# Loading the first half of K in float32 over SyncE's queue and casting it on chip, in a fused attention and FFN kernel

## The chip, the cores and the metric

The kernel runs on one core of one Trainium2 chip. The metric is the device time of one execution in microseconds (us). Three runs of the kernel before took 511.74, 512.51 and 513.07 us; the median is 512.51 us. Engine names: PE is TensorE (PEld its weight loads), DVE VectorE, ACT ScalarE, POOL GpSimd, SP SyncE.

## The reference

```
k_proj = einsum('ks,bhsd->bhkd', E, k)          # E, F: 64 x 1024
v_proj = einsum('ks,bhsd->bhkd', F, v)          # q, k, v: 8 x 8 x 1024 x 64
scores = q @ k_proj^T / sqrt(64)                # per batch and head: 1024 x 64
attn   = softmax(scores, axis=-1)
x      = (attn @ v_proj), heads side by side    # 8192 x 512
h      = relu(x @ w_in)                         # w_in: 512 x 2048
out    = (h * h) @ w_out                        # w_out: 2048 x 512, out in float32
```

All inputs and the output are float32 in memory. The kernel computes in bfloat16 with float32 accumulation.

## The kernel before, in words

**Batches.** The eight batches are worked one after another. For each, the attention result xT (heads by tokens, bfloat16) feeds an FFN in two chunks of 512 tokens. While PE runs the FFN of batch b, the attention stages of batch b+1 and the projections of batch b+2 are put between its matmuls by a plan written out by hand (`at(step, ...)`, L461 to L514): the FFN is a generator of steps, and after step n the stages planned for n are issued. The order on PE is the order of the program text; the other engines' orders follow from it.

**Opening.** Batch 0 has no earlier FFN to hide under, so its attention runs ahead of all else (L428 to L455). E is loaded in float32 by SP (L87) into a tile of `soft_pool` with the tag "rs" (three buffers, also used by the inverse of the softmax sums), cast to bfloat16 by DVE (L429), and transposed on PE (`projection`, L132, with a DVE copy at L138). `project_k(0)` (L191 to L197) multiplies ET with the first four heads of K (8 matmuls at L194), `project_k(1)` does the other four. `transpose_q_chunk` (L227), `transpose_k` (L210), `chunk_scores` (L322), `chunk_sums` (L328), `project_v` (L199) and `chunk_values` (L333) follow for the first chunk of 512 tokens in groups of four heads. `warm(n)` (L141) issues n matmuls on zeros.

**First FFN chunk of batch 0.** `Ffn.steps` with `cold` set: the first matmuls are at L358 (input weights, `w_in`), ReLU on ACT (L354) and square on DVE (L355), then second matmuls (L364) with `w_out` in four pieces. The last piece, `w_out_131` in the profile, is first used at step 23, where the plan also holds the second chunk's scores.

**Queues.** Nearly all loads are issued by POOL (`load`, L75), since POOL's transfers cast float32 to bfloat16 on the way. Their order at the start is: K heads 0 to 3, Q heads 0 to 3 (half of the tokens), F, K heads 4 to 7, Q heads 4 to 7 (half), V heads 0 to 3, V heads 4 to 7, then five pieces of w_in, three of w_out, the rest of Q, the last of w_out, and the whole K, V and Q of the batches 1 and 2. At most eight of POOL's transfers are under way: the ninth waits for the first to land, the tenth for the second, and so on. SP issues E, and later the stores of the output (L373, the first at 44.02 us) and the transposing DMAs.

The part around the change reads:

```
for g in range(2):
    load(K0[:, half[g]], tokens(k, 0, h=half[g]))
    load(Q0[:, half[g], 0:4, :], tokens(q, 0, h=half[g], i=slice(0, 4)))
    if g == 0:
        make_identity(nc, ident[:])
        load(f_bf[:], F[:])
```

Of the kernel before, what the change touches and what calls it, by code (L numbers as in the profile page):

```python
# [8 lines left out]
P = 128  # L9
F32 = mybir.dt.float32  # L10
# [8 lines left out]
def kernel(  # L19
# [11 lines left out]
    nc = tc.nc  # L31

    B, H, S, D = q.shape
# [5 lines left out]
    NI = 8  # L39
# [18 lines left out]
    soft_pool = ctx.enter_context(tc.tile_pool(name="soft", bufs=3))  # L58
# [10 lines left out]
    def bank(shape=(P, 512), dtype=F32):  # L69
        return fps.tile(list(shape), dtype, tag="bank", name="ps_bank")  # L70

    def tokens(src, b, h=slice(None), i=slice(None)):
        return src[b].rearrange("h (p i) d -> p h i d", i=NI)[:, h, i, :]

    def load(t, src):  # L75
        return nc.gpsimd.dma_start(t, src)  # L76
# [9 lines left out]
    e_f32 = soft_pool.tile([KP, S], F32, tag="rs", name="e_f32")  # L86
    nc.sync.dma_start(e_f32[:], E[:])  # L87

    K0, Q0, V0 = (qkv_pool.tile([P, H, NI, D], BF16, name=n) for n in ("K_sb", "Q_sb", "V_sb"))
    f_bf = soft_pool.tile([KP, S], BF16, tag="expT", name="f_bf")  # L90
    half = (slice(0, 4), slice(4, 8))
    ident = const_pool.tile([P, P], BF16, name="ident")
    for g in range(2):
        load(K0[:, half[g]], tokens(k, 0, h=half[g]))
        load(Q0[:, half[g], 0:4, :], tokens(q, 0, h=half[g], i=slice(0, 4)))
        if g == 0:
            make_identity(nc, ident[:])
            load(f_bf[:], F[:])
# [13 lines left out]
    for lo, hi in W_IN_PIECES:  # L112
        t = wpool.tile([P, NCB, (hi - lo) * P], BF16, name=f"w_in_{lo}")
# [4 lines left out]
    for j in range(WP):  # L118
        if j == WP - 1:
            load(Q0[:, :, 4:8, :], tokens(q, 0, i=slice(4, 8)))  # L120
        t = wpool.tile([P, fn, DM], BF16, name=f"w_out_{j}")
# [10 lines left out]
    def projection(name, e_bf):  # L132
        ps = bank([P, NI, KP], BF16)
        view = e_bf[:].rearrange("k (p i) -> k i p", i=NI)
        for i in range(NI):
            nc.tensor.transpose(ps[:, i, :], view[:, i, :], ident[0:KP, 0:KP])
        t = const_pool.tile([P, NI, KP], BF16, name=name)
        nc.vector.tensor_copy(t[:], ps[:])  # L138
        return t

    def warm(n):  # L141

        ps = bank()
        for _ in range(n):
            nc.tensor.matmul(ps[:], lhsT=zeros[:, 0:P], rhs=zeros[:], start=True, stop=True)
# [281 lines left out]
    with tc.manual_schedule(engines={PE}):  # L427
        e_bf = soft_pool.tile([KP, S], BF16, tag="expT", name="e_bf")  # L428
        nc.vector.tensor_copy(e_bf[:], e_f32[:])  # L429
        warm(8)  # L430
        ET = projection("ET", e_bf)
        warm(4)
        att = Attention(0)
        att.project_k(0)
        warm(1)
        att.transpose_q_chunk(0, Q0, 0)
        att.transpose_k((0,))
        warm(3)
        att.chunk_scores(0, 0)
        FT = projection("FT", f_bf)  # L440
        warm(3)
        att.project_k(1)
        att.chunk_sums(0, 0)
        att.transpose_q_chunk(0, Q0, 1)
        att.transpose_k((1,))
        warm(2)
        att.chunk_scores(0, 1)
        warm(2)
        att.project_v(0)
        warm(1)  # L450
        att.chunk_sums(0, 1)
        att.chunk_values(0, 0)
        warm(1)
        att.project_v(1)
        att.chunk_values(0, 1)  # L455

        coming = None
        for b in range(B):
            plan = {}

            def at(step, fn, *args, **kwargs):  # L461
                plan.setdefault(step, []).append(lambda: fn(*args, **kwargs))

            if b == 0:
                at(21, att.transpose_q_chunk, 1, Q0, 0)
                at(21, att.transpose_q_chunk, 1, Q0, 1)
                at(23, att.chunk_scores, 1, 0)
                at(23, att.chunk_scores, 1, 1)
                at(25, att.sums, 0)
                at(27, att.chunk_values, 1, 0)  # L470
                at(27, att.chunk_values, 1, 1)
                nxt = Attention(1)
                nxt.load()
            if b + 1 < B:
                if b + 2 < B:
                    coming = Attention(b + 2)
                    coming.load()
                if b == 0:
                    at(36, nxt.project)
                    at(39, nxt.transpose_q, 0)  # L480
                    at(39, nxt.transpose_q, 1)
                    at(39, nxt.transpose_k)
                    at(41, nxt.scores, 0)
                    at(41, nxt.scores, 1)
                    at(44, nxt.transpose_q, 2)
                    at(44, nxt.transpose_q, 3)
                    at(45, nxt.sums, 0)
                    at(48, nxt.values, 0, True)
                    at(48, nxt.scores, 2)
                    at(51, nxt.values, 1)  # L490
                    at(51, nxt.scores, 3)
                    at(55, nxt.sums, 2)
                    at(55, nxt.values, 2)
                    at(55, nxt.values, 3, True)
                else:
                    at(14, nxt.scores, 0)
                    at(14, nxt.scores, 1)
                    at(18, nxt.sums, 0)
                    at(18, nxt.values, 0, True)
                    at(18, nxt.scores, 2)  # L500
                    at(27, nxt.values, 1)
                    at(27, nxt.scores, 3)
                    at(49, nxt.sums, 2)
                    at(49, nxt.values, 2)
                    at(49, nxt.values, 3, True)
                if b + 2 < B:
                    if b == 0:
                        at(61, coming.project)
                        at(63, coming.transpose_q_dma)
                        at(64, coming.transpose_k)  # L510
                    else:
                        at(27, coming.project)
                        at(30, coming.transpose_q_dma)
                        at(29, coming.transpose_k_dma)  # L514
            for step, _ in enumerate(Ffn(att, b == 0).steps(), 1):
                for stage in plan.pop(step, []):
                    stage()
            assert not plan, plan
            att, nxt = nxt, coming
# [30 lines left out]
```

## Time and profile before

| what | value |
|---|---|
| profiled execution, device time | 511.74 us |
| its span, first to last instruction | 510.0 us |
| median of three runs | 512.51 us |
| PE busy | 497.0 us, 97% |
| ACT, DVE, POOL busy | 272.4, 216.7, 32.0 us |
| DMA, POOL's queue | 29.49 MB in 30880 packets |
| DMA, SP's queue | 23.99 MB in 36928 packets |
| read from memory | 59.24 MB |

The profile is of one execution, which was also the quickest of the three; 1.74 us of its time lie outside the span. The bytes of POOL's queue are counted in bfloat16, after the cast: twice 29.49 MB and E's 0.26 MB make the 59.24 MB that were read. A rate of 208 GB/s on that queue is thus 416 GB/s of reading.

A row of the timeline gives start, length, engine, line, operation, tiles and count; in brackets is how long the engine sat idle before it and what ended that. A POOL or SP row of a DMA is its issue; its landing is told by the view of the tile.

### The profile page before, as it was taken

To read this page: it belongs to the slowest core of one execution; us is meant where nothing else is said; L and a number is where in the kernel's file an instruction comes from. 1 tells how busy PE (TensorE), PEld (TensorE's weight loads), DVE (VectorE), ACT (ScalarE), POOL (GpSimd) and SP (SyncE) were. 2 spreads that over 40 slices of the span, in tenths; PEclk is the share of its full clock that TensorE was granted. 3 is DMA by queue.
4 is the path that set the end of the run, shared out by engine and by line. 5 is a ranking of instruction groups with operands and counts; after the bars stand their busy time and mean duration, and the time that the engine had idled before them with its cause. 6 is when DMAs were issued, how large, how long until landed. Compare 5 with 4: busy or idle time off the path is not lost.

```text
span 510.0 us, 6889 instructions
## 1 busy us (share of the span) xinstructions
PE 497.0 (97%) x2710; PEld 222.8 (44%) x2761; DVE 216.7 (42%) x437; ACT 272.4 (53%) x411; POOL 32.0 (6%) x44
## 2 busy tenths in 40 slices
PE   8799999999999999999999999999999999999997
PEld 4344444444444444444444444444444444444444
DVE  2442766444434445235452345444443443522130
ACT  2564484664718556374645736366472755544351
POOL 7320100121000020001000000000000000000000
PEclk9999999999999999999999999999999999999999
DMA  9999999899996199104931060101102011010102
GB/s 156 204 205 222 226 207 202 132 220 207 195 217 125 56 185 201 65 0 126 181 78 42 17 160 1 62 22 42 53 1 82 1 41 42 31 54 21 63 0 82
DMA packets 67840, 53.92 MB, mean 106 GB/s; under 512 B 29152, under 2 KB 59616, under 8 KB 67808
## 3 DMA queue, kind: packets, MB, share of 16 engines
q0 software_dynamic: 30880, 29.49, 36.8%
q1 hardware_dynamic: 36928, 23.99, 17.5%
q8 instruction: 21, 0.34, 0.3%
q14 instruction: 11, 0.09, 0.1%
HBM read 59.24 MB, written 16.78 MB: 149 GB/s over the span
## 4 chain that ended last, share of the span: by engine, by line
PE 88%; DMA 7%; issue 2%; POOL 1%; ACT 1%; DVE 1%; POOLq 0%; ACTq 0%
PE ps_bank L364 41%; PE ps_bank L358 40%; DMA w_out_131<-in_moe_w_out_dram 4%; DMA w_in_116<-in_moe_w_in_dram 3%; PE ps_bank L185 2%; PE ps_att L256 1%; PE ps_att L290 1%; PE ps_att L312 1%; PE ps_bank L312 1%; DVE rs L300 0%; PE ps_bank L241 0%; DVE xT L341 0%; POOL K_sb L76 0%; POOL V_sb L76 0%; ACT expT L270 0%
## 5 line engine op out<-in xcount | busy, mean ns | idle before, releaser
L355 DVE TENSOR_TENSOR hsq<-h_relu 128x512 bf16<-128x512 bf16 x256 | 108.9, 426 | 192.9 <-ACT h_relu L354 192.0
L354 ACT ACTIVATE h_relu<-ps_bank 128x512 bf16<-128x512 f32 x256 | 151.7, 599 | 69.3 <-PE ps_bank L358 69.2
L364 PEld LDWEIGHTS <-hsq 128*128 128x128 bf16 x1040 | 99.5, 98 | 123.6 <-issue 9.3
L371 ACT COPY o_sb<-ps_bank 128x512 f32<-128x512 f32 (+1 forms) x65 | 37.6, 579 | 119.7 <-PE ps_bank L364 110.9
L364 PE MATMUL ps_bank<-w_out_124,hsq 128*128 128x512 bf16 (+1 forms) x257 | 65.6, 376 | 0.2
L364 PE MATMUL ps_bank<-w_out_131,hsq 128*128 128x512 bf16 (+1 forms) x251 | 64.1, 376 | 1.4 <-issue 1.1
L364 PE MATMUL ps_bank<-w_out_128,hsq 128*128 128x512 bf16 (+1 forms) x252 | 64.3, 376 | 1.1 <-issue 1.0
L364 PE MATMUL ps_bank<-w_out_126,hsq 128*128 128x512 bf16 (+1 forms) x249 | 64.2, 376 | 1.1 <-issue 0.8
L300 DVE COPY rs<-rs 32x1024 f32<-32x1024 f32 x60 | 41.3, 689 | 47.2 <-ACT rs L295 45.8
L358 PE MATMUL ps_bank<-xT,w_in_122 128*128 128x512 bf16 x255 | 58.9, 380 | 0.0
L358 PE MATMUL ps_bank<-xT,w_in_118 128*128 128x512 bf16 x250 | 57.7, 380 | 0.4
L358 PE MATMUL ps_bank<-xT,w_in_120 128*128 128x512 bf16 x247 | 57.4, 379 | 0.4
L270 ACT ACTIVATE expT<-ps_att 128x1024 bf16<-128x1024 f32 x32 | 31.8, 1024 | 18.1 <-PE ps_att L256 18.1
L358 PEld LDWEIGHTS <-w_in_120 128*128 128x128 bf16 x256 | 24.9, 98 | 30.4 <-issue 0.4
L358 PEld LDWEIGHTS <-w_in_118 128*128 128x128 bf16 x256 | 24.9, 98 | 30.2 <-issue 0.4
L358 PEld LDWEIGHTS <-w_in_122 128*128 128x128 bf16 x256 | 24.4, 98 | 31.1 <-issue 2.7
L358 PE MATMUL ps_bank<-xT,w_in_114 128*128 128x512 bf16 x128 | 30.6, 379 | 0.3 <-DVE xT L341 0.2
L358 PE MATMUL ps_bank<-xT,w_in_116 128*128 128x512 bf16 x126 | 30.0, 379 | 0.1
L294 ACT ACTIVATE rs<-ps_att 128x1024 f32<-128x1024 f32 x15 | 15.3, 1023 | 12.7 <-PE ps_att L290 12.7
L316 DVE TENSOR_TENSOR xT<-ps_att,rs 128x512 bf16<-128x512 f32 x28 | 18.1, 686 | 8.7 <-PE ps_att L312 8.4
L358 PEld LDWEIGHTS <-w_in_114 128*128 128x128 bf16 x128 | 12.4, 98 | 15.6 <-issue 1.3
L358 PEld LDWEIGHTS <-w_in_116 128*128 128x128 bf16 x128 | 12.5, 98 | 15.2 <-issue 0.2
(71 smaller groups left out, 233.9 us busy)
## 6 DMA issues: line engine op xcount, KB each, us to landing
out_dram<-o_sb SPq DMA_DIRECT2D x63, 256.0 KB, 2.0
K_sb<-in_k_dram POOLq DMA_DIRECT2D x7, 1024.0 KB, 22.1
V_sb<-in_v_dram POOLq DMA_DIRECT2D x7, 1024.0 KB, 26.7
Q_sb<-in_q_dram POOLq DMA_DIRECT2D x7, 1024.0 KB, 15.0
K_sb<-in_k_dram POOLq DMA_DIRECT2D x2, 512.0 KB, 7.1
V_sb<-in_v_dram POOLq DMA_DIRECT2D x2, 512.0 KB, 12.0
Q_sb<-in_q_dram POOLq DMA_DIRECT2D x2, 256.0 KB, 7.6
w_in_118<-in_moe_w_in_dram POOLq DMA_DIRECT2D x1, 512.0 KB, 15.5
```

Of the source, the lines that this page charges most:

```text
L185: nc.tensor.matmul(ps[LO, :], lhsT=ET[:, i, :], rhs=self.K[:, :, i, :], start=f, stop=l)
L256: nc.tensor.matmul(ps[o, par], lhsT=self.kT[r, h % 4, h // 4, :], rhs=self.qT[r, h, n, :], start=True, stop=True)
L270: nc.scalar.activation(e[:], ps[:], AF.Exp, scale=SCALE)
L294: nc.scalar.activation(rs[1][:], ps[:], AF.Ln)
L300: nc.vector.tensor_copy(rs[j][lack:lack + 32], rs[j][have:have + 32])
L312: nc.tensor.matmul(ps_x[par][o], lhsT=self.vp[r, 2 * pr + a, :], rhs=e[r, par], start=True, stop=True)
L316: nc.vector.tensor_tensor(out=self.xT[:, pr, :, par], in0=ps_x[par].rearrange("p (c t) -> p c t", c=2), in1=rs[:, par].rearrange("p (c t) ...
L354: nc.scalar.activation(r[:], ps[:], AF.Relu)
L355: nc.vector.tensor_tensor(out=self.hsq[c][:, fb, :], in0=r[:], in1=r[:], op=ALU.mult)
L358: nc.tensor.matmul(ps[:], lhsT=w_in_blk(cb, fb), rhs=self.xT[:, cb, c].rearrange("p a t -> p (a t)"), start=(cb == 0), stop=(cb == NCB - 1),)
L364: nc.tensor.matmul(ps[:, m], lhsT=self.hsq[c][:, fb, tb * P:(tb + 1) * P], rhs=w_out_blk(fb)[:, m], start=(fb == 0), stop=(fb == NFB - 1),)
L371: nc.scalar.copy(o[:, m], ps[:, m])
```

## The change

The first half of K (heads 0 to 3 of batch 0, 1 MB of float32) is no longer loaded by POOL with a cast. SP issues it behind E in two float32 transfers of two heads each, into two tiles of the tag "rs". DVE casts the first (heads 0 and 1) ahead of its copy of ET, ACT the second (heads 2 and 3) ahead of its copy of the projected K, into the same K tile. POOL's first transfer is now Q. All else is as before.

```
@@ -86,12 +86,19 @@
+    k_f32 = []
+    for j in range(2):
+        t = soft_pool.tile([P, 2, NI, D], F32, tag="rs", name="k_f32")
+        nc.sync.dma_start(t[:], tokens(k, 0, h=slice(2 * j, 2 * j + 2)))
+        k_f32.append(t)
...
     for g in range(2):
-        load(K0[:, half[g]], tokens(k, 0, h=half[g]))
+        if g == 1:
+            load(K0[:, half[g]], tokens(k, 0, h=half[g]))
...
         nc.vector.tensor_copy(e_bf[:], e_f32[:])
+        nc.vector.tensor_copy(K0[:, 0:2], k_f32[0][:])
+        nc.scalar.copy(K0[:, 2:4], k_f32[1][:])
         warm(8)
```

## Prediction

> **What bounds the kernel now.** I read the page's first lines, then the timeline of the opening, the waits, and the DMA rate in fine slices.
>
> ```profile
> PE 497.0 (97%) x2710; PEld 222.8 (44%) x2761; DVE 216.7 (42%) x437; ACT 272.4 (53%) x411; POOL 32.0 (6%) x44
> ```
>
> PE is busy for 497.0 of 510.0 us, so nearly all of its idle time can only lie in the opening, the part that the change touches. The timeline there:
>
> ```profile
> 0.74 0.57 SPq L87 DMA_DIRECT2D e_f_91<-in_E_dram  x1
> 1.25 0.89 POOL L76 DMA_DIRECT2D K_sb<-in_k_dram  x1 [0.80 <-POOLq L534]
> 2.14 0.76 POOL L76 DMA_DIRECT2D Q_sb<-in_q_dram  x1
> ...
> 4.37 0.81 DVE L429 CAST e_bf<-e_f_91 64x1024 bf16<-64x1024 f32 x1 [3.15 <-DMA e_f_91<-in_E_dram]
> ...
> 5.95 0.42 DVE L138 COPY ET<-ps_bank 128x512 bf16<-128x512 bf16 x1 [0.77 <-PE ps_bank L136]
> ...
> 7.32 1.03 PE L194 MATMUL ps_bank<-K_sb,ET 128*64 128x256 bf16 x8 [0.44 <-DMA K_sb<-in_k_dram]
> ...
> 14.62 1.06 ACT L276 ACTIVATE rs<-rs 128x1024 f32<-128x1024 f32 x1
> ...
> 19.74 1.06 PE L204 MATMUL ps_bank<-V_sb,FT 128*64 128x256 bf16 x16 [1.44 <-DMA V_sb<-in_v_dram]
> ...
> 42.35 1.02 PE L364 MATMUL ps_bank<-w_out_131,hsq 128*128 128x512 bf16 x4 [0.19 <-DMA w_out_131<-in_moe_w_out_dram]
> ```
>
> PE waits for three transfers in turn: 0.44 us for the first half of K (7.32), 1.44 us for the last half of V (19.74), and 0.19 us for the last piece of w_out (42.35). The last row decides. From 19.74 to 42.35 PE's own work and the stream of loads run side by side, and they arrive within 0.19 us of each other. To end sooner the kernel needs both: PE earlier at the FFN, and w_out_131 (issued 22.1, landing 20.2 us later at 42.3) earlier. After 42.35 no transfer holds PE up again. So the change is worth the **smaller** of two advances, x of PE and y of the stream. The stream is full almost from the start, shown in 40 slices of 0.1 us from 2 to 6 us:
>
> ```profile
> GB/s 82 328 205 0 0 41 0 246 287 492 410 369 236 72 62 21 10 61 61 143 154 174 215 184 184 205 236 195 205 225 205 195 195 225 164 143 154 184 174 184
> ```
>
> E's float32 comes at about 400 GB/s around 3 us. POOL's transfers count bytes after the cast, so their 205 means 410 GB/s read: the same ceiling. Between them is a hole, 3.3 to 4.0 us, with a mean of 61.
>
> **The change, part by part.**
>
> *The stream, y.* Bytes read stay the same: 1.05 MB of K takes 2.5 to 2.6 us at 410 GB/s either way. What can move is idle time. The K transfers stand in SP's queue right behind E; E's bytes begin about 1.3 us after its issue, and at 0.57 us each SP has issued both K transfers by 2.45, so their bytes follow E's without a break, while POOL's Q begins about when K did, near 3.3. The hole closes: 0.7 us x (1 - 61/208) = 0.5 us. Against it: float32 written at full width, and two queues mixed. The nearest row is a store beside POOL's loads: near 48 us, six slices of 0.25 us stand at a mean of 282 GB/s; a store's 262 KB over 1.5 us is 175 of it, which leaves 107 of loads, or 214 read: 389 moved in place of 410, 5% lost, and the two queues share about evenly. Over some 4 us of mixing that is 0.2 us, and 0.3 at the 8% by which 4 to 12 us (190 GB/s) falls short of 205 to 209 later. I take 0.15, since K comes first and mixes for less. Upward bound: the hole and also this early shortfall made good, 0.5 + 8% of 8 us = 1.1. So y is 0.35; if the hole stays and the 0.3 is lost, -0.3; at best +1.1.
>
> The Trainium skill, "DMA: Bandwidth & Descriptors", Rules for kernel authors, speaks against the change: spreading transfers over several issuing engines gives no bandwidth, since all share 16 DMA engines; only issue time is saved. By it y is 0, for the 0.89 us of POOL's issue saved is not on the path. It is a rule for a running stream; the hole above is a starting one, and I go by the hole.
>
> *PE's way to the FFN, x.* Removed: the 0.44 us wait for K at 7.32. Added: K's second tile, then ACT's cast, and only then L194. Landing: bytes from 3.2. If K has the engines alone, they end at 5.8; if it shares evenly with Q (0.52 MB read), at 7.1. E landed at 0.74 + 3.6 = 4.3, about 0.8 us after its bulk ended, so K lands at 6.6 to 7.9. The cast of 128x1024 on ACT isn't in the trace; the nearest row, L276 of that shape from SBUF, is 1.06 us. L194 starts at 7.7 to 9.0 instead of 7.32, d = 0.4 to 1.7; I take 1.0, the middle: the store's row speaks for even sharing, K's place ahead of Q for the engines alone. DVE's cast of the first tile (the e_bf row, 0.81 us: time goes by elements in a row) stands ahead of the ET copy, which PE needs: at a landing of 5.0 to 6.6 it ends at 5.8 to 7.4 and ET at 6.2 to 7.9, before ACT's cast ends. Behind ACT's cast is only the copy of the projected K (L174), which needs L194 anyway.
>
> From L194 to the wait for V, PE runs back to back (2.95 us busy of 9 to 12, 5.78 of 12 to 18.3), so d is handed on, less about 0.1 where it stood for other landings. It arrives before V's last half at 18.3 + 0.9 = 19.2; V landed at 19.7. So the 1.44 us idle swallows the delay. V moves with the stream: 19.35. Also, V's second half came 3.7 us after the first (15.98 to 19.7) where 0.52 MB at 208 GB/s take 2.5; one 16 KB instruction fetch lies in 13 to 26 us and may have held one engine up. If it falls elsewhere, V lands near 18.2 and PE's 19.2 decides. So x is 0.4 to 0.5, between 0 (d = 1.6) and 1.4 (d = 0).
>
> *The rest, at nothing.* POOL has one transfer fewer and issues each of the others up to 0.89 us earlier; the eight-under-way rule keeps pairing the same transfers from the tenth on, so the stream is fed as before. SP's next work is the store at 44.02. The two new tiles take the "rs" buffers, first wanted again at 13.57, after both casts. Warm-up matmuls are unchanged. If cover is gone, ACT's cast costs 1.06.
>
> *Sum.* min(x, y) = 0.35: 511.74 - 0.35 = 511.4 for the profiled execution, the fastest of three. On the median 512.51, 0.77 above it, that is **512.1 us**.
>
> **Rivals**, on the median too.
>
> 1. *Nothing gained:* y is 0, as w_out_131 lands when it did; mixing eats the hole, or the stall of one engine by an instruction fetch sets the landing. For it: the landing is set by the slowest of 16 engines. PE gains at most the 0.19 of its wait: 512.4. Against it: the hole is real idle time of all engines.
> 2. *Slower: K late.* If POOL's packets get two turns in three, K crawls from 3.2 at half its rate or less, 205 GB/s: 5.1 us, bytes end at 8.3, landed 9.1, cast done 10.2, L194 at 10.3, d = 3.0. It decides from d = 1.6, L194 at about 8.9. Price d - 1.6 = 1.4: 513.9. For it: stores between 44 and 54 us land 5.4 to 7.0 us after issue, held behind POOL's loads, against 2.0 in the middle of all. Against: K enters engines that hold nothing of POOL's yet. With it comes a second price: PE idles from about 6.9 to 10.3. The trace shows 1.4 us of idle (18.3 to 19.7) at a granted clock of 1.00; the first eight matmuls of 512 columns take 3.59 us, later four 1.04, so a fallen clock would double PE's work for some us: up to 2 more, 515.9.
> 3. *More gained:* y = 1.1 and V not held up, d at 0.4: 511.4.
>
> The Trainium skill, "TensorE: Matmul & The Clock Gate", What's actually happening, lets the clock fall only after an idle window of some 3.4 us. By it the forecast's gap (about 7 to 8.3) leaves the clock alone, and rival 2 stands at its edge. No row here shows a fall.
>
> **How the numbers follow.** Forecast 0.45, rival 1 0.22, rival 2 0.18, rival 3 0.15. Runs of one kernel spread from 511.74 to 513.07, so about 0.3% (1.5 us) is what can be told from no change. The range takes in rival 3 less half of that spread (511.4 - 0.6) and rival 2's first price with a little of it: 510.8 to 514.2. Faster by over 0.3% needs more than every advance found: 0.06, by rival 3 and spread. Slower by over 0.3%, above 514.0, takes rival 2 at its dear end: 0.13. Within: 0.81.
>
> **What would show it.** In the profile after: no hole at 3.3 to 4.0 us in the DMA slices; K's second tile landing at 6.6 to 7.9; ACT's cast about 1.06 us; L194 at 7.7 to 9.0; L204's second batch at 18.9 to 19.5; the wait at w_out_131 still there, and its row at about 42.0. It would be wrong if L194 came after 9, if w_out_131 landed no earlier, or if w_out_131 no longer ended any wait and the time still moved.

## The result and the profile after

| kernel | median | lowest to highest | runs |
|---|---|---|---|
| before | 513.13 us | 511.74 to 513.28 | 6 |
| after | 514.75 us | 514.05 to 516.43 | 6 |

The changed kernel is slower: ratio **1.0041**, 95% interval 1.0023 to 1.0059. That is 1.6 us on the medians, and 2.3 us between the two profiled executions, each of them the quickest of its kernel (514.05 and 511.74).

PE's busy slices on the page of before, then the span, PE's busy slices and the granted clock on the page of after (40 slices each, in tenths):

```profile
PE   8799999999999999999999999999999999999997
```
```profile
span 512.3 us, 6897 instructions
...
PE   5999999999999999999999999999999999999997
...
PEclk7999999999999999999999999999999999999999
```

PE's slices differ in the first two alone, so the 2.3 us lie in the opening. Its timeline answers to the rows that the prediction showed of before:

```profile
1.37 0.57 SPq L92 DMA_DIRECT2D k_f_93<-in_k_dram  x1
1.99 0.45 SPq L92 DMA_DIRECT2D k_f_95<-in_k_dram  x1
...
5.61 0.69 DVE L437 CAST K_sb<-k_f_93 128x1024 bf16<-128x1024 f32 x1 [0.42 <-DMA k_f_93<-in_k_dram]
...
9.24 1.04 ACT L438 CAST K_sb<-k_f_95 128x1024 bf16<-128x1024 f32 x1 [7.21 <-DMA k_f_95<-in_k_dram]
10.34 1.86 PE L201 MATMUL ps_bank<-K_sb,ET 128*64 128x256 bf16 x8 [3.45 <-ACT K_sb L438]
...
16.52 1.06 PE L201 MATMUL ps_bank<-K_sb,ET 128*64 128x256 bf16 x8
...
22.58 1.06 PE L211 MATMUL ps_bank<-V_sb,FT 128*64 128x256 bf16 x16
...
44.85 1.03 PE L371 MATMUL ps_bank<-w_out_134,hsq 128*128 128x512 bf16 x4
```

The two tiles of K were issued 0.6 us apart and landed 3.6 us apart: DVE's cast of the first waited until 5.61, ACT's of the second until 9.24. PE then stood still for 3.45 us, and began the first K product at 10.34 instead of 7.32. Its eight matmuls took 1.86 us, not 1.03: the clock had fallen. The last two rows have no bracket. Nothing waits for V or for the last piece of w_out any more; PE comes later than both.

The windows of after show the clock; the columns are the window, its length, PE, PEld, DVE, ACT and POOL busy, the granted clock, the DMA share and GB/s. They are cut at the instants at which the clock's record changes:

```profile
4.07:7.49 3.42, 2.08 (x14) 0.98 (x13) 1.71 (x3) 0.00 (x0) 3.42 (x5) 1.00 1.21 293
7.49:10.90 3.41, 0.56 (x3) 0.48 (x3) 0.00 (x0) 1.04 (x1) 2.08 (x3) 0.50 1.19 233
10.90:14.31 3.41, 3.41 (x22) 2.03 (x20) 1.09 (x3) 0.36 (x1) 1.48 (x2) 0.50 1.32 202
14.31:17.72 3.41, 3.36 (x33) 1.90 (x32) 0.74 (x4) 1.02 (x1) 0.74 (x1) 1.00 1.26 204
```

Half clock lasts two windows, 7.49 to 14.31. In the first PE mostly waits; in the second it works at half speed throughout. So the product of the second half of K, which in before stands at 12.11,

```profile
12.11 1.06 PE L194 MATMUL ps_bank<-K_sb,ET 128*64 128x256 bf16 x8
```

is at 16.52: the 3.02 us have become 4.41. By the second product with V (22.58 against 19.74) it is 2.84, because V's idle time of 1.44 us is swallowed, and at the last piece of w_out 2.50 (44.85 against 42.35). From there on the offset stays: 2.50 up to about 150 us and 2.45 from 175 us to the last of these matmuls, as PE hardly idles there.

The DMA rate of after from 2 to 6 us, in slices of 0.1 us:

```profile
GB/s 82 369 164 0 41 0 0 0 369 410 369 451 389 226 164 246 225 184 246 205 205 307 369 369 410 430 410 389 410 348 236 195 210 195 189 195 205 200 200 225
```

Up to 4.9 us all of this is float32, so 410 is full rate. The hole of before, 3.3 to 4.0, is half filled: a mean of 213 GB/s. From 4.9 on the bytes are POOL's, counted after the cast, so 200 is full rate again.

### The profile page after: what moved, and what is told of

Same layout as the page of the kernel before. It is cut to its first block, busy times and chain, and to the rows that moved or that the text cites. A ratio compares the mean times of both kernels' runs of the same rounds, so it can differ in the third digit from the quotient of the medians.

```text
span 512.3 us, 6897 instructions
## 1 busy us (share of the span) xinstructions
PE 497.9 (97%) x2710; PEld 223.8 (44%) x2761; DVE 217.2 (42%) x438; ACT 273.7 (53%) x412; POOL 31.4 (6%) x43
## 4 chain that ended last, share of the span: by engine, by line
PE 93%; issue 2%; DVE 1%; DMA 1%; ACT 1%; SPq 0%; DVEq 0%; ACTq 0%
PE ps_bank L365 43%; PE ps_bank L371 41%; PE ps_bank L192 2%; PE ps_att L263 1%; DMA k_f_95<-in_k_dram 1%; PE ps_att L319 1%; PE ps_att L297 1%; DVE xT L348 1%; PE ps_bank L319 1%; PE ps_bank L201 1%; PE ps_bank L152 1%; PE ps_bank L238 0%; PE ps_bank L248 0%; ACT expT L277 0%; DVE rs L307 0%
```

## The experiments

The theory, from the two traces: the second tile of K lands late because SP's queue has to take turns with POOL's loads (the cause), and PE's wait for it costs twice, once as delay and once as lost clock. The rivals: float32 or the casts themselves cost; Q's issue ahead of the tile alone is to blame; the lost clock does not matter, or is all that matters.

**The second tile through ACT's queue** (e1).

```
-        nc.sync.dma_start(t[:], tokens(k, 0, h=slice(2 * j, 2 * j + 2)))
+        (nc.sync if j == 0 else nc.scalar).dma_start(t[:], tokens(k, 0, h=slice(2 * j, 2 * j + 2)))
```

> Only the issuing engine of the second K tile changes: ACT's queue, at about 0.75 us, in place of SP's third place at 1.99. Theory (order of arrival): the tile came late, at 9.2 us, because its packets reached the DMA engines just behind those of POOL's Q and then took turns with POOL's. Ahead of Q it should land at 6.0 to 7.0, the first L194-type matmul (L201) start at 7.1 to 8.1, the granted clock stay at 1.00 and the time come back to within 0.5 us of before (0.999 to 1.001). Rival (rate): float32 in 2 KB packets over a hardware queue is slow in itself, and E and the first tile beside it make it worse: the tile lands at 8.5 or later and the time stays about 1.003 to 1.004 of before.

512.58 us (511.82 to 514.33, 12 runs), ratio 0.9995 [0.9983, 1.0008]. The loss is gone in the median, yet not in the execution that was profiled, its slowest. The timeline of that one:

```profile
4.63 1.04 ACT L438 CAST K_sb<-k_f 128x1024 bf16<-128x1024 f32 x1 [2.61 <-DMA k_f<-in_k_dram]
6.09 0.68 DVE L436 CAST e_bf<-e_f 64x1024 bf16<-64x1024 f32 x1 [4.88 <-DMA e_f<-in_E_dram]
9.17 0.69 DVE L437 CAST K_sb<-k_f 128x1024 bf16<-128x1024 f32 x1 [2.40 <-DMA k_f<-in_k_dram]
```

By the starts of the casts, ACT's tile lands first, at 4.6; E lands by 6.1, against 4.5 in after; and now SP's tile of K is the late one, at 9.2. In both kernels the third float32 transfer to land is the late one. Neither the size of the tiles nor the number of casts changed, so the casts are not the price of the change.

**Twenty warm-up matmuls** ahead of the first K product in place of four (e2).

```
-        warm(4)
+        warm(20)
```

> The changed kernel with 20 warm-up matmuls instead of 4 ahead of project_k(0), so that PE works through the wait. The landing of K and the cast stay: L201 at 10.3. Theory: the late K costs 3.0 us at L201 and the fallen clock another 1.4 by the second half of K; without the fall the FFN starts at about 23.1 in place of 24.5 and the time is 1.3 to 1.5 us below the changed kernel, about 1.001 to 1.002 of before. Rival (clock): the fallen clock is the whole loss, since V's wait swallows the rest; then the time is within 0.3 us of before. If the clock plays no part, the time stays at 1.003 to 1.004.

514.18 us (513.04 to 514.73), ratio 1.0023 [1.0011, 1.0034]. In the profiled execution the clock rose only at 10.47, so the twenty took 6.75 us and put the product itself off to 12.55, past K. They are too many to tell the clock's share; n5 below has fewer.

**Q behind the identity** (e3): POOL's first load is moved behind `make_identity`.

```
-        load(Q0[:, half[g], 0:4, :], tokens(q, 0, h=half[g], i=slice(0, 4)))
         if g == 0:
             make_identity(nc, ident[:])
+        load(Q0[:, half[g], 0:4, :], tokens(q, 0, h=half[g], i=slice(0, 4)))
+        if g == 0:
             load(f_bf[:], F[:])
```

> POOL issues its first Q load behind the making of the identity, some 0.5 us later than in the changed kernel; nothing else moves. Theory (order of arrival): the second K tile's packets now enter before Q's and follow the first tile's: landing at 6.3 to 7.2 in place of 9.2, L201 at 7.4 to 8.3, clock 1.00, time 0.999 to 1.001 of before. Rival (rate): half a microsecond of head start changes the landing by no more than that, 8.7 or later, and the time stays at about 1.003.

514.63 us (513.94 to 515.82), ratio 1.0035 [1.0022, 1.0048]. It tells nothing of the order: Q's issue moved only from 1.25 to 1.28 us. It stands as a second measurement of after: the second tile landed at 9.46, though in its profile DVE cast K's first tile ahead of E.

**Heads 2 and 3 back to POOL** (e4): SP loads one float32 tile, POOL the other two heads, as its first load, with the cast.

```
-    for j in range(2):
+    for j in range(1):
...
-        if g == 1:
-            load(K0[:, half[g]], tokens(k, 0, h=half[g]))
+        h0 = slice(2, 4) if g == 0 else half[1]
+        load(K0[:, h0], tokens(k, 0, h=h0))
...
-        nc.scalar.copy(K0[:, 2:4], k_f32[1][:])
```

> Only heads 0 and 1 come in float32 over SP, cast by DVE; heads 2 and 3 come by POOL with its cast, as its first load; ACT's cast is gone. Theory: POOL's piece follows the float32 piece in the engines and lands at 6.3 to 7.0, L201 starts at 6.9 to 7.1, at or before the 7.32 of before. The stream of loads, a little ahead as the hole after E is filled, sets the end: 0.2 to 0.5 us below before, 0.999 to 1.000. Rival (any float32 K beside POOL is a loss): L201 at 8 or later and the time above 1.002.

512.16 us (511.31 to 514.26, 12 runs), ratio **0.9985 [0.997, 0.9999]**: faster than before, by 0.77 us on the medians, with an interval that just clears 1. The timeline of its profiled execution (513.28 us, one of its slower ones):

```profile
5.80 0.92 DVE L437 CAST K_sb<-k_f 128x1024 bf16<-128x1024 f32 x1 [0.66 <-DMA k_f<-in_k_dram]
...
7.10 1.06 PE L201 MATMUL ps_bank<-K_sb,ET 128*64 128x256 bf16 x8 [0.25 <-DVE ET L145]
...
19.49 1.06 PE L211 MATMUL ps_bank<-V_sb,FT 128*64 128x256 bf16 x16 [1.34 <-DMA V_sb<-in_v_dram]
42.35 1.02 PE L371 MATMUL ps_bank<-w_out,hsq 128*128 128x512 bf16 x4 [0.43 <-DMA w_out<-in_moe_w_out_dram]
```

PE waits for no K at all, only for ET. The waits for V and w_out are back, and the last row is at 42.35, exactly where before had it: the stream decides again. So one float32 tile and its cast are harmless, and the second tile behind it is the harm. Where the 0.77 us come from, this profile does not show, as its opening ends no sooner than in the profile of before.

**Q 0.4 us later** (e5): a memset on POOL ahead of its first load.

```
+    pause = const_pool.tile([P, 1024], F32, name="pause")
+    nc.gpsimd.memset(pause[:], 0.0)
```

> The changed kernel with POOL filling a 128x1024 float32 tile of zeros ahead of its first load, so that Q and all behind it are issued about 1 us later or more. (The earlier attempt at this moved Q's issue by 0.03 us only and told nothing.) Theory (order of arrival): the second K tile's packets now reach the engines before Q's and follow the first tile's without the pause of 1 us: landing at 6.3 to 7.5 in place of 9.2, L201 at 7.4 to 8.6. The time is then 0.999 to 1.001 of before, unless the stream runs dry behind K. Rival (the hardware queue): SP's third transfer is late whatever POOL does, landing 8.5 or later, time 1.003 or more.

513.88 us (512.52 to 514.9), ratio 1.0009 [0.9993, 1.0024]. Q's issue moved to 1.63, and the second tile began right behind the first; but in the profiled execution ACT's cast still had to wait until 9.48:

```profile
9.48 1.04 ACT L441 CAST K_sb<-k_f 128x1024 bf16<-128x1024 f32 x1 [7.46 <-DMA k_f<-in_k_dram]
10.57 1.86 PE L204 MATMUL ps_bank<-K_sb,ET 128*64 128x256 bf16 x8 [3.77 <-ACT K_sb L441]
```

This does not settle the order, though. The profiled execution is the slowest of the twelve, and its packet records have thirteen packets of K that took 0.36 to 1.55 us each, between 4.6 and 6.9 us, where 0.08 to 0.10 is usual and after has none above 0.18. All but 21 of the second tile's 256 packets had begun by 7.6 us; the last began at 8.7. By the median e5 lies where the theory of order had it, at 1.0009, below e3 (1.0035) and after (1.0041), with intervals that all but part. That speaks for a share of the order in the loss.

**K late without float32** (e6): the kernel before, with POOL's load of the first half of K put behind Q and F.

```
     for g in range(2):
-        load(K0[:, half[g]], tokens(k, 0, h=half[g]))
         load(Q0[:, half[g], 0:4, :], tokens(q, 0, h=half[g], i=slice(0, 4)))
         if g == 0:
             make_identity(nc, ident[:])
             load(f_bf[:], F[:])
+        load(K0[:, half[g]], tokens(k, 0, h=half[g]))
```

> The kernel before, all loads by POOL with the cast, only that K's first half is issued behind Q and F in place of ahead of them: no float32 K, no cast on ACT or DVE. 0.79 MB more is read ahead of it, 1.9 us at 410 GB/s, so it lands at about 9.2. Theory: the loss is that of a late first K and of nothing else; L194 starts at 9.2 to 9.4, PE idles 2.4 us, and the time is 1.001 to 1.004 of before, by whether the clock falls. Rival (the float32 path, with its casts and its 2 KB packets, is what costs): the time stays within 0.001 of before.

514.51 us (513.04 to 515.45), ratio 1.0023 [1.0006, 1.0039], so 1.80 us above the median of before in its job (512.71). Its first product, in the timeline:

```profile
9.30 1.87 PE L196 MATMUL ps_bank<-K_sb,ET 128*64 128x256 bf16 x8 [2.41 <-DMA K_sb<-in_k_dram]
```

A product at 9.3 and at half clock (1.87) costs about what the change costs, with no float32, no cast and no second queue. The late K is enough.

**Six output buffers** in place of four, in before (e7) and after (e8).

```
-    out_pool = ctx.enter_context(tc.tile_pool(name="outp", bufs=4))
+    out_pool = ctx.enter_context(tc.tile_pool(name="outp", bufs=6))
```

> The kernel before with six output buffers in place of four. In several profiles PE stands still for 1.4 us at about 152 us, as ACT's copies of the output wait for stores that SP holds behind its transposing DMA; in the profile of before it did not. Theory: this second place is where runs of one kernel differ, and where a late kernel gets part of its loss back. Without the wait the median is 0.5 to 1.5 us below before (0.997 to 0.999). Rival: the place is of no weight, the time the same within 0.001.

> The changed kernel with six output buffers. Theory: it was 2.5 us late behind the opening in its profile, but its median is only 1.6 to 1.8 us above before, since being late spares it part of the wait at 152 us. With that wait gone from both, the two differ by the whole of the opening: this one is 2.2 to 2.6 us above the run with six buffers before the change, so 1.002 to 1.003 of before. Rival (the wait is independent of the lateness): both come down by the same amount and the difference stays at 1.7.

512.61 (511.63 to 513.41) and 514.91 us (514.3 to 515.54), ratios 0.9983 [0.9967, 0.9998] and 1.0034 [1.0021, 1.0048]. Their difference, 2.30 us, lies where it was expected, but the intervals are too wide to say that the buffers took a stall away from before alone. What the pair does add: in e7's profile POOL's load of K landed later than in before, the product came at 8.37, and the clock fell for one window. So the kernel before has such executions too, and 511.74 is not its usual time. In that profile the last piece of w_out was late as well: PE waited 0.61 us for it, to 43.80.

**Transposes on PE.** The next kernels do the later batches' transposes of Q and K on PE, where the others do them by SP's transposing DMAs. All four get the same edit, which adds about 12 us after the opening, and are compared with one another:

```
-        def transpose_k_dma(self):
-            nc.sync.dma_start_transpose(...)
+        def transpose_k_late(self):
+            self.transpose_k()
...
+        def transpose_q_late(self):
+            for pr in range(NPAIR):
+                self.transpose_q(pr)
```

With it are before (n1), after (n2), the split of e4 (n3), and after with POOL paused by four memsets, one ahead of Q's issue and three ahead of F's (n4):

```
+    pause = const_pool.tile([P, 1024], F32, name="pause")
+    for _ in range(4):
+        nc.gpsimd.memset(pause[:], 0.0)
```

> The kernel before with the transposing DMA of the later batches done by PE and DVE instead (the opening has none and is untouched). It is the base for the three beside it, and takes the transposes off SP's queue, behind which the stores waited. Some 7 x 32 transposes of 65 ns or less come onto PE: 8 to 16 us slower than before, ratio 1.015 to 1.03. Theory: the wait at 152 us is gone and the executions lie within some 2 us of each other.

> The changed kernel with the same replacement. Theory: what the change costs is the opening alone, the whole of it, since no later wait gives part back: 2.0 to 2.6 us above the same replacement of the kernel before (0.004 to 0.005 of ratio). Rival: the cost is bound up with SP's queue later on (its two more transfers shift the order of SP's semaphores); without the transposing DMA there the two are within 0.7 us.

> Heads 0 and 1 in float32 over SP and cast by DVE, heads 2 and 3 as POOL's first load, with the same replacement. Theory: K is complete by 7.0 and the opening is no later than before: 0 to 1.0 us below the same replacement of the kernel before. Rival (the first result of the split was chance): 0 to 0.7 us above it.

> The changed kernel with the same replacement, and with POOL filling the 128x1024 tile four times ahead of its first load, so that Q and all behind it are issued some 3 us later. Holding Q back by 0.4 us took away the pause before the second K tile but not its late landing; so order of arrival isn't the whole cause. Theory (turns): the tile shares each DMA engine with POOL's loads packet by packet, and its last packets on the slowest engines are late. With POOL out of the way it lands at 5.8 to 7.3, and L201 starts at 6.9 to 8.4. All loads behind are late, so the end is still 1 to 3 us above the same replacement of the kernel before. Rival (the hardware queue): it lands at 8.5 or later with POOL's queue empty too.

| kernel | median | lowest to highest, runs | ratio to before | against n1 |
|---|---|---|---|---|
| n1, before | 524.89 us | 524.53 to 527.61, 5 | 1.0240 [1.0214, 1.0265] | |
| n2, after | 527.86 us | 527.05 to 528.05, 4 | 1.0285 [1.0262, 1.0307] | +2.97 |
| n3, split | 524.51 us | 524.07 to 524.67, 4 | 1.0221 [1.0199, 1.0243] | -0.38 |
| n4, POOL paused | 526.16 us | 525.53 to 529.34, 6 | 1.0267 [1.0239, 1.0294] | +1.27 |

The loss of the change is still there, somewhat larger than expected, and the split again removes it. That the split is faster than before, as e4 had it, is not confirmed: the intervals of n3 and n1 overlap widely. N4 is the one that tells why the tile is late. Its timeline:

```profile
5.67 0.86 POOL L76 DMA_DIRECT2D f_bf<-in_F_dram  x1
5.73 0.69 DVE L438 CAST K_sb<-k_f 128x1024 bf16<-128x1024 f32 x1 [4.52 <-DMA k_f<-in_k_dram]
6.34 0.68 DVE L437 CAST e_bf<-e_f 64x1024 bf16<-64x1024 f32 x1
...
7.57 1.05 ACT L439 CAST K_sb<-k_f 128x1024 bf16<-128x1024 f32 x1 [5.55 <-DMA k_f<-in_k_dram]
...
9.52 1.69 PE L205 MATMUL ps_bank<-K_sb,ET 128*64 128x256 bf16 x8
```

With F issued at 5.67 instead of 2.28, and all behind it later, ACT's cast starts at 7.57: the second tile comes 1.7 us sooner than in after, 0.3 behind the theory's 5.8 to 7.3 and clear of the rival's 8.5. This is a single execution, but in all seven other profiles with both tiles in SP's queue the cast of the second starts at 9.2 or later. The packet records of after and n4 show the difference; the number of packets begun in each 0.4 us, SP's of 2 KB and POOL's of 512 bytes or more:

| from | after, SP | after, POOL | n4, SP | n4, POOL |
|---|---|---|---|---|
| 4.8 us | 41 | 68 | 78 | 0 |
| 5.2 | 0 | 154 | 72 | 11 |
| 5.6 | 1 | 158 | 61 | 16 |
| 6.0 | 39 | 69 | 46 | 51 |
| 6.4 | 49 | 46 | 20 | 112 |
| 6.8 | 43 | 32 | 4 | 146 |
| 7.2 | 27 | 26 | 0 | 140 |
| 7.6 | 29 | 23 | 0 | 65 |
| 8.0 | 43 | 32 | 0 | 34 |
| 8.4 | 25 | 51 | 0 | 25 |

In after, the second tile stands still for 0.9 us, 5.1 to 6.0, while POOL's Q runs alone, and then goes packet by packet with POOL's Q, F and second half of K. From 6.4 to 8.4 it moves 191 packets of 2 KB, 196 GB/s, half of the 390 that are read. In n4 the tile starts right behind the first one and has Q alone beside it: its packets run from 4.9 to 7.2, and F's begin at 7.5. In after they run from 6.0 to 8.8. So 1.0 of the 1.6 us between the two ends is the later start, and 0.6 the slower flow. The Trainium skill, "DMA: Bandwidth & Descriptors", Queues, rings and completion order, says that each DMA engine goes round the queues that have work for it, packet by packet. From 6.4 to 8.4 after's trace has 191 packets of SP to 159 of POOL, which is near to that; the 0.9 us without a turn for SP are not explained by it, and stay open.

The product in n4 came at 9.52, not at the 6.9 to 8.4 of the theory, for another reason: DVE took the cast of K ahead of E's, so ET was late, and PE's gap dropped the clock (granted 0.50 from 7.43 to 10.84). So n4 tells of the landing and not of the full price.

**The clock's share** (n5, n6): n2 with ten warm-up matmuls in place of four, few enough to end ahead of the cast at either clock, and n1 with eight.

```
-        warm(4)
+        warm(10)
```

> The changed kernel with the later batches' transposes on PE, and ten matmuls on zeros in place of four ahead of the first K product. They take 2.1 us at full clock and 4.2 at half, so they end by 8.0 or 10.1 us, before ACT's cast ends near 10.3 to 10.6, and can't put the product off. If half clock is a part of the loss (about 1.4 us between the two K products where it fell), this lies 0.3 to 1.2 us below the same kernel with four (527.86 us, so 526.7 to 527.6), and the product still starts at 10.2 to 10.7. Rival, that the late landing alone is the loss: within 0.3 us of 527.86.

> The kernel before with the later batches' transposes on PE, and eight matmuls on zeros in place of four ahead of the first K product. At full clock they end at 7.6, at half clock at 9.3 us. If the clock decides the spread of the kernel before (524.5 to 527.6 us), the slow end goes: all runs within 1.5 us, median 524.3 to 525.5. Rival, that the spread comes from K's landing alone: median up by 0.5 to 1.5 us (525.4 to 526.4), since the added matmuls stand ahead of the product, and the spread stays at 3 us.

N5: **525.78 us** (525.47 to 527.82, 5 runs), ratio 1.0257 [1.0235, 1.0280]. Its timeline:

```profile
5.92 2.33 PE L152 MATMUL ps_bank<-zeros 128*128 128x512 bf16 x10
9.22 1.04 ACT L435 CAST K_sb<-k_f 128x1024 bf16<-128x1024 f32 x1 [7.20 <-DMA k_f<-in_k_dram]
10.31 1.03 PE L201 MATMUL ps_bank<-K_sb,ET 128*64 128x256 bf16 x8 [2.06 <-ACT K_sb L435]
```

The same kernel with four, n2, and below it the second K product of n5:

```profile
10.62 1.86 PE L201 MATMUL ps_bank<-K_sb,ET 128*64 128x256 bf16 x8 [2.87 <-ACT K_sb L435]
...
17.46 1.06 PE L201 MATMUL ps_bank<-K_sb,ET 128*64 128x256 bf16 x8
```
```profile
14.94 1.06 PE L201 MATMUL ps_bank<-K_sb,ET 128*64 128x256 bf16 x8
```

K is as late as in after (9.22 against 9.24, product at 10.31 against 10.34), but the product runs at full clock, 1.03 us. From the first K product to the second n5 takes 4.63 us, before 4.79, after 6.18 and n2 6.84: the low clock costs 1.4 us there in after (against before) and 2.2 in n2 (against n5). In n5 the clock rose at 5.21, ahead of the added matmuls, so that part of this pair is chance; what they can have done is keep it up. Four of its five runs lie below all of n2's. By the medians n5 takes away 2.08 of the 2.97 us, and what is left above n1, 0.89, is put down to the late tile. By the ratios to the kernel before of each job it is 1.4 and 0.9 (0.0028 and 0.0017 of 513); the intervals of n2 and n5 overlap a little, so the sizes are rough; by both the clock is the larger part.

N6: 525.27 us (524.44 to 526.22, 4 runs), ratio 1.0237 [1.0217, 1.0257], the same as n1's 1.0240. The spread of 1.8 lies between the two expectations, so whether n1's one run at 527.61 was the clock alone stays open.

## Why the prediction was wrong

The forecast was 512.1 us; the time is 514.75, above the range's end at 514.2. The path was rival 2's, which had 0.18.

1. **The step that failed: "K lands at 6.6 to 7.9".** It landed at 9.2. The sharing itself was right: SP's queue got half. But the upper bound let K share with Q alone (0.52 MB read) from 3.2 us on. The trace of after shows three things more: the first 0.8 us of K run at half rate with nothing else moving (3.3 to 4.1); the second tile waits for 0.9 us behind Q, 5.1 to 6.0; and F and the other half of K, issued by POOL close behind Q, take its other turns up to 8.8. From 6.0, 0.52 MB at 196 GB/s are 2.7 us; the last packet ends at 8.8, and the tile landed by 9.2. N4 weighs the last two. It has the bound's own case, Q alone beside the tile and no pause, and its cast starts at 7.57, inside the forecast's 6.6 to 7.9; against it the tile of after starts 1.0 us later and flows 0.6 us longer. Rival 2 had 9.1, L194 at 10.3 and d = 3.0; measured 9.2, 10.34 (now L201) and 3.02. That it is so close is partly luck: it took 205 GB/s from 3.2 to 8.3 throughout, by two turns in three for POOL, and K came at half rate, at full rate, not at all, and at half rate again. What was held against it, that "K enters engines that hold nothing of POOL's yet", holds for the first tile (5.6) and fails for the second.
2. **The clock.** Rival 2 priced it as up to 2 us, and the forecast had none. N5 puts it at 1.4 to 2.1, and the way from the first K product to the second at 1.4 in after. I had weighed the rule of the Trainium skill ("TensorE: Matmul & The Clock Gate", What's actually happening) as a gap of 3.4 us, with the forecast's gap well inside. The length of the window agrees with the trace, 3.41 us. That it must be idle does not: in after the clock fell at 7.49, 0.6 us after PE had stopped, at the end of a window in which PE was busy for 2.08 of 3.42 us. Even with a K product at 8.37 (e7) it fell.
3. **The stream, y = 0.35.** Right in size and wrong in its parts: w_out_134 was issued at 20.8 and landed 21.2 us later, at 42.0, so 0.3 sooner than 42.3. By the packet records, POOL's bytes doubled, after has read 0.05 MB more than before by 4 us and 0.15 MB more by 14 us, which is 0.1 and 0.4 us at 410 GB/s. So the hole gave 0.1 us and not 0.5, and no loss by mixing is seen, where 0.15 was taken off; the rest came between 4 and 14 us, which the prediction had as an upward bound alone. That the sum fits is luck. It bought nothing, since PE came at 44.85. "The wait at w_out_131 still there" was wrong: no wait is there. The rule of the Trainium skill ("DMA: Bandwidth & Descriptors", Rules for kernel authors), by which y is 0, missed those 0.3 us and was right on what they are worth.
4. **The casts.** ACT 1.04 us measured, 1.06 taken; DVE 0.69 against 0.81. They cost nothing beyond the landing that they wait for, except that ACT's 1.04 stands between K and PE.
5. **V swallows the delay.** Right: 4.41 us at the second K product are 2.84 at the second V product, 1.57 gone, where 1.44 of idle were to be had. It was priced against a delay of 1.0 and met 4.4.
6. **The base.** The forecast was put on the profiled execution of before. That one was the quickest of its runs: K early, the clock up from 5.32 to the end. Profiles of the same opening in e7 and n1 show K at 8.4 to 8.5 and a fall of the clock, so before meets a late K and a low clock at times too. That may be why the medians differ by 1.6 us and the profiles by 2.3, but it is not shown: of the 90 runs of before beside the experiments 33 have a mean granted clock of 0.997 or less, which is a fall for one window or more, and as a group they are not clearly slower than the others (means 513.12 and 512.94 us).

## What to carry to other kernels

When a transfer that starts the work is moved to a second queue, ask not whether the DMA engines have a hole for it, but which loads of the other queue will be there when its last byte is due: it gets turns, not precedence. Split it so that each queue has its part of what must land first ahead of its other loads; here that version, e4, is 0.15% below before, barely clear of noise, where the whole move loses 0.41%. And price an idle gap of PE in the warm-up twice, as delay and as lost clock; here ten matmuls on zeros that end before the data arrive (n5) lowered the median by 1.4 to 2.1 us.

## What was not expected of the hardware

**The clock's first window.** PE's busy time in the 3.41 us after the clock rose, from the windows of the twelve profiles in which it rose before 6 us:

| kernel | rose at | PE busy in the next 3.41 us | then |
|---|---|---|---|
| before | 5.32 us | 2.97 us | stayed |
| n5 | 5.21 | 2.94 | stayed |
| e4 | 4.90 | 2.86 | stayed |
| n6 | 4.18 | 2.74 | stayed |
| after | 4.07 | 2.08 | fell at 7.49 |
| n1 | 4.32 | 1.95 | fell at 7.73 |
| e6 | 4.57 | 1.83 | fell at 7.99 |
| e7 | 4.57 | 1.82 | fell at 7.98 |
| e1 | 4.64 | 1.37 | fell at 8.06 |
| e5 | 5.68 | 1.13 | fell at 9.09 |
| e3 | 4.94 | 0.95 | fell at 8.35 |
| n4 | 4.02 | 0.81 | fell at 7.43 |

So the clock fell with 2.08 us of work or less and stayed with 2.74 or more. A fixed share does not explain it all: in n5's next window PE was busy for only 1.72, and the clock stayed.

```profile
5.21:8.62 3.41, 2.94 (x18) 1.57 (x19) 1.07 (x3) 0.00 (x0) 2.83 (x4) 1.00 1.18 265
8.62:12.03 3.41, 1.72 (x17) 1.31 (x16) 0.42 (x1) 1.24 (x2) 1.48 (x2) 1.00 1.29 201
```

**A clock of 1.00 that is none.** In n2 and e8 the first record of the clock is at 16.14 and 16.82 us, and the profile fills in 1.00 ahead of it. The durations tell otherwise. The row of n2:

```profile
12.82 1.06 PE L236 MATMUL ps_bank<-ident,Q_sb 128*128 128x128 bf16 x8
```

The same eight take 0.62 us in before. So the clock there rose late instead of falling. The price was much the same or higher: n2's second K product is at 17.46, after's at 16.52.

**A slow start of the second transfer.** The 2 KB packets of K's first tile take about 160 ns each from 3.3 to 4.0 us and 84 from 4.4, with nothing else under way (205 and 410 GB/s). The hole of before lies at the same place. It is not so in every execution: in e4 such packets take 84 to 115 ns. No experiment looked for its cause.
